# Second expert in a recurrence and mixture-of-experts kernel: three resident slabs in place of four streamed, with the planner's numbers set anew

## The chip, the cores and the metric

The kernel runs on one core of a Trainium2 chip. The metric is the device time of one execution in microseconds (us). Before the change three runs gave a median of 2320.58 us (2311.55 to 2326.86).

## What is computed

Three layers follow one another. The first is a recurrence over 768 tokens for 4 x 8 heads with a 40 x 40 state each, the second a mixture of eight experts whose weights P come from a Sinkhorn iteration over all 3072 tokens, the third one wide layer with an ELU. The reference, cut:

```python
for t in range(S):                                   # S = 768
    y[:, :, t] = np.einsum('bhd,bhde->bhe', rt, state)
    Sa = np.einsum('bhde,bhe->bhd', state, at)
    state_decay = state * wt[:, :, None, :] - np.einsum('bhd,bhe->bhde', Sa, bt)
    state = state_decay + np.einsum('bhd,bhe->bhde', vt, kt)
...
for e in range(E):                                   # 8 experts, D = 320, F = 1024
    h = np.maximum(x @ w1[e], 0.0)
    out += P[:, e:e + 1] * (h @ w2[e])
...
g = np.where(h > 0.0, h, alpha * (np.exp(np.minimum(h, 0.0)) - 1.0))   # h = x @ w_in, 2048 wide
return g @ w_out
```

## The kernel before

**Recurrence phase.** The 768 steps are cut into 12 chunks of 64 tokens (`NC`), and a chunk of all batches and heads gives 256 rows of x. A chunk is computed in matrix form on 16 head pairs in 4 groups. Its steps, in the names of the code: `scan`, `recip0` to `recip2`, `amul`, `bkmul` (VectorE and ScalarE); `gmm`, `at_t`, `kb_t` (TensorE); the inverse of a triangular matrix in 31 pairs `t_mul`, `t_add` on VectorE, which write the tiles TMP and U; then for each group in turn the state chain `y0mm` (R,SN), `qsmm` (matmul RHS,PT, then RHS<-bank,QM on VectorE), `ysmm` (matmul RHS,KB, then STMP, ST and Y on VectorE) and `trmm` (ident,ST). The matmul of the last group's `ysmm` ends a chunk: in this text the end of every fourth group of RHS,KB matmuls.

**Experts under the recurrence.** TensorE would have gaps in that chain, so the first experts' matmuls are put into them. An expert has 8 slabs of weights (128 of its 1024 hidden columns each, 352 KB). A slab is loaded by SP into one of two staging buffers `wst`, copied by ScalarE into one of 11 ring slots (`NSLOT`; tiles w), and the rest of the split into two planes is a subtraction that reads `wst` and the slot (line 596). This text calls one slab against the 256 rows of a chunk a **half step**: 8 matmuls of 256 columns (`mm1`), ReLU and split on ScalarE and VectorE (tiles hh, hl), and 6 matmuls of 320 columns each for one of two row blocks of 128, 12 in all for a full step on 512 rows (`mm2`). Expert 0 stays in slots 0 to 7 for all chunks (`moe0_items`). Of expert 1 slabs 0 to 3 are streamed for each of the chunks 0 to 9 through slots 8 to 10 (`moe1_items`, `stream_load`, `stream_split`, lists `STREAM` and `PASSES`): 40 loads, 40 copies on ScalarE and 40 subtractions on GpSimd. After chunk 9 the three slots are filled with slabs 0 to 2 once more, for the units: 3 of each again. Half steps per chunk: 8 and 4.

**What sets the order.** A planner (`class Order`) records each step's instructions, links them by the tiles they touch and sets the order of all engines ahead of time by a list schedule with prices for each instruction. Its ranks are moved by the table `AHEAD` and by `SLACK`, `FILL`, `FED` and `SAME`; the expert items (`item`) have a low rank on TensorE. When no expert item is open, it sets 128 x 128 matmuls on a tile of ones into gaps. Each engine then runs its instructions strictly in the order written. Expert items that the planner has not begun when the recurrence work is placed are kept in `left`.

**Behind the recurrence.** `moe0_rest` replays `left` and computes chunk 11's expert 0. The Sinkhorn steps hang in a queue `hookq` and are issued between matmuls by `tick`. As slots come free, `post_m2` puts `wsplit` of the slab 11 places on into the queue `late`; each pop issues a copy on ScalarE, a subtraction on GpSimd and the load of the next slab but one on SP. Then come the **units**: one slab against 512 rows (8 matmuls of 512 columns, 12 of 320), first what is left of expert 1, then experts 2 to 7 and the ELU layer in the same form (two sets): `units`, 8 + 5 x 4 = 28 for expert 1 and 384 for the other eight sets. The second matmuls of a unit run three units behind the first (`LAG`). `LEFT` lists the 512-row blocks whose earlier expert results are added from memory later on, 6 + 5.

Of the kernel before, what the change touches and what calls it, by code (L numbers as in the profile page):

```python
# [26 lines left out]
STREAM = [4, 4, 4, 4, 4]  # L27
PASSES = [f for c in range(10) for f in range(STREAM[c // 2])]
# [9 lines left out]
AHEAD = {"tnt": 60, "emm": 60, "t21": 20, "pmm": 60, "y0mm": 60, "qsmm": 60, "ysmm": 60, "trmm": -60, "st_copy": 60, "rvmm": 60, "load_vt": 60, "u_out": 60, "u_in": 60, "l_out": 20, "l_in": 100, "gmm": 40, "load_v": 20, "wsplit": -30}  # L38
# [15 lines left out]
class Order:  # L54
# [283 lines left out]
    SLACK, QUEUE, FILL, FED, SAME = 200.0, 1000.0, 0.0, 2000.0, 0.0  # L338
# [193 lines left out]
def kernel(  # L532
# [50 lines left out]
    wload_next, wlimit = [0], [NF - 1]  # L583

    def wload(i):
        while wload_next[0] <= min(i, wlimit[0]):
# [13 lines left out]
    def stream_load(k):  # L600
        if k < len(PASSES):
            SP.dma_start(out=wst[k % 2], in_=wslab[NF + PASSES[k]])

    def stream_split(k):
        if k < len(PASSES):
# [343 lines left out]
    def moe1_items(c):  # L949
        x = XS[c % 2]  # L950
        if c == 0:
            for k in range(2):
                stream_load(k)
            for k in range(3):
                stream_split(k)
                yield
        n = STREAM[c // 2]
        for f in range(n + 1):
            k = sum(STREAM[i // 2] for i in range(c)) + f
            if f < n:  # L960
# [384 lines left out]
```

## Time and profile before

| | us |
|---|---|
| median of the runs | 2320.58 |
| the profiled execution's own time | 2315.57 |
| its span | 2313.9 |
| TensorE busy | 2211.1 (96%) |
| VectorE busy | 1241.1 (54%) |
| ScalarE busy | 904.1 (39%) |
| GpSimd busy | 308.5 (13%) |

PE is TensorE, PEld its weight loads, DVE VectorE, ACT ScalarE, POOL GpSimd, SP the engine that issues nearly all transfers (SPq its queue). Times in the rows are us from the span's start. The profile gives one line (336) to all that the planner places, so its groups are told apart by the names of their tiles. A busy PE counts a matmul at a low clock as fully as one at a high clock; the granted clock (PEclk, 1.00 for the upper level of 2.4 GHz, 0.50 for the lower of 1.2) stands beside it.

### The profile page before, as it was taken

What the parts mean: (1) busy time and instruction counts of PE and PEld (TensorE: products, weight loads), DVE (VectorE), ACT (ScalarE), POOL (GpSimd) and SP (SyncE); (2) the same over time, 40 slices, a digit from 0 to 9 for tenths busy, and PEclk for the clock granted to TensorE, in tenths of its full rate; (3) what the DMA queues carried; (4) which work ended last, traced back from release to release, by engine and by line L of the source; (5) the groups of instructions that cost most, each with busy time, mean ns of one, the idle gap of its engine ahead of it and who ended that gap; (6) DMA issues with size and microseconds to landing.
All of it is one profiled execution on the core that took longest, in us unless ns stands there. A gap on an engine that the chain in (4) does not pass through costs nothing.

```text
span 2313.9 us, 42293 instructions
## 1 busy us (share of the span) xinstructions
PE 2211.1 (96%) x17586; PEld 1997.3 (86%) x17586; DVE 1241.1 (54%) x2518; ACT 904.1 (39%) x1897; POOL 308.5 (13%) x319
## 2 busy tenths in 40 slices
PE   6997999999999899999999999999999999999997
PEld 6876888888888889999999999999999998999997
DVE  7887477777775454556555432222222334556665
ACT  3554565565555222112112112112112224777665
POOL 2212222212221211002002002002002002001000
PEclk8877999999999899999999999999999999999999
DMA  3444444444443441113122101001001001000000
GB/s 100 111 127 109 122 119 130 121 123 126 118 119 89 140 132 47 61 61 110 61 61 88 38 23 51 1 1 51 1 1 51 1 1 51 1 1 20 19 24 29
DMA packets 171400, 152.65 MB, mean 66 GB/s; under 512 B 107648, under 2 KB 142336, under 8 KB 170240
## 3 DMA queue, kind: packets, MB, share of 16 engines
q1 hardware_dynamic: 170940, 149.53, 23.2%
q8 instruction: 140, 2.29, 0.4%
q14 instruction: 60, 0.49, 0.1%
q10 hardware_dynamic: 260, 0.33, 0.0%
HBM read 114.83 MB, written 35.00 MB: 65 GB/s over the span
## 4 chain that ended last, share of the span: by engine, by line
PE 85%; DVE 10%; issue 2%; ACT 1%; DMA 1%; POOL 0%; SPq 0%; DVEq 0%; ACTq 0%; POOLq 0%
PE bank L616 32%; PE bank L336 22%; PE bank L626 10%; PE bank L625 10%; PE bank L624 10%; DVE TMP L336 3%; DVE U L336 2%; DVE RHS L336 2%; DVE Y L336 0%; DVE ST L336 0%; DVE STMP L336 0%; PE bank L1149 0%; DMA wst<-in_wslab_dram 0%; DVE A L336 0%; ACT A L336 0%
## 5 line engine op out<-in xcount | busy, mean ns | idle before, releaser
L616 PE MATMUL bank<-X,w 128*128 128x512 f32 (+1 forms) x3360 | 829.6, 388 | 0.0
L616 PEld LDWEIGHTS bank<-X,w 128*128 128x128 f32 x3360 | 606.3, 188 | 103.4
L620 DVE SCALAR_TENSOR_TENSOR hl<-bank,hh 128x512 fp32r<-128x512 f32 x320 | 220.2, 689 | 607.7 <-ACT hh L619 607.6
L626 PE MATMUL bank<-w,hl 128*128 128x320 f32 x1664 | 515.0, 309 | 0.8 <-DVE hl L1143 0.8
L624 PE MATMUL bank<-w,hh 128*128 128x320 f32 x1664 | 514.0, 309 | 0.7 <-ACT hh L1142 0.7
L625 PE MATMUL bank<-w,hh 128*128 128x320 f32 x1664 | 514.3, 309 | 0.0
L619 ACT ACTIVATE hh<-bank 128x512 fp32r<-128x512 f32 x320 | 191.7, 599 | 814.0 <-PE bank L616 809.4
L624 PEld LDWEIGHTS bank<-w,hh 128*128 128x128 f32 x1664 | 313.3, 188 | 16.8 <-ACT hh L1142 1.1
L625 PEld LDWEIGHTS bank<-w,hh 128*128 128x128 f32 x1664 | 313.2, 188 | 15.6
L626 PEld LDWEIGHTS bank<-w,hl 128*128 128x128 f32 x1664 | 313.0, 188 | 1.3 <-DVE hl L1143 1.3
L596 POOL TENSOR_TENSOR w<-wst,w 128x704 fp32r<-128x704 f32 x69 | 118.6, 1720 | 1245.4 <-ACT w L595 1227.9
L336 PE MATMUL bank<-XS,w 128*128 128x256 f32 x1024 | 157.8, 302 | 0.0
L336 PEld LDWEIGHTS bank<-XS,w 128*128 128x128 f32 x1024 | 139.2, 202 | 6.2 <-issue 2.8
L369 DVE SCALAR_TENSOR_TENSOR NX<-EX,NX 128x512 f32<-128x512 f32 (+1 forms) x104 | 68.6, 660 | 135.0 <-ACT NX L368 134.6
L336 DVE TENSOR_TENSOR TMP<-U,LD 128x126 f32<-128x126 f32 (+22 forms) x372 | 133.2, 358 | 14.1 <-DMA BK<-in_wakb_dram 2.7
L336 PE MATMUL bank<-w,hh 128*128 128x320 f32 x512 | 126.3, 333 | 0.1
L336 DVE TENSOR_TENSOR U<-U,TMP 128x126 f32<-128x126 f32 (+22 forms) x372 | 111.8, 301 | 11.4
L1163 DVE SCALAR_TENSOR_TENSOR OUT<-bank,pp,OUT 128x320 f32<-128x320 f32 x144 | 69.2, 543 | 54.1 <-PE bank L626 54.1
L336 POOL TENSOR_TENSOR w<-wst,w 128x704 fp32r<-128x704 f32 x43 | 73.7, 1716 | 174.2 <-ACT w L336 88.5
L366 ACT ACTIVATE NX<-bank 128x512 f32<-128x512 f32 (+1 forms) x104 | 58.8, 565 | 83.6 <-PE bank L616 80.7
L336 DVE SCALAR_TENSOR_TENSOR hl<-bank,hh 128x512 fp32r<-128x512 f32 (+1 forms) x84 | 47.1, 560 | 78.8 <-ACT hh L336 78.5
L336 PEld LDWEIGHTS bank<-w,hh 128*128 128x128 f32 x512 | 85.2, 196 | 4.8 <-issue 2.1
(135 smaller groups left out, 2464.2 us busy)
## 6 DMA issues: line engine op xcount, KB each, us to landing
wst<-in_wslab_dram SPq DMA_DIRECT2D x104, 352.0 KB
RAW<-in_wslab_dram SPq DMA_DIRECT2D x32, 352.0 KB
BK<-in_wakb_dram SPq DMA_DIRECT2D x24, 320.0 KB
x_d<-XS SPq DMA_DIRECT2D x12, 640.0 KB
X<-x_d SPq DMA_DIRECT2D x12, 640.0 KB
ye_d<-YE SPq DMA_DIRECT2D x22, 320.0 KB
XS<-ye_d SPq DMA_DIRECT2D x11, 640.0 KB
LD<-l_d SPq DMA_DIRECT2D x24, 256.0 KB
```

The source lines that it names most:

```text
L336: getattr(self.engines[s.eng], method)(*args, **kwargs)
L366: nc.scalar.activation(out=n, in_=h, func=AF.Relu, scale=-1.0)
L369: nc.vector.scalar_tensor_tensor(out=n, in0=e, scalar=1.0, in1=n, op0=ALU.add, op1=ALU.mult)
L596: (V if i < NF else P).tensor_tensor(out=w[:, 1, :], in0=st, in1=fv(w[:, 0, :]), op=ALU.subtract)
L616: PE.matmul(ps, w[:, pl, c0:c0 + 128], x[:, m, :], start=(t == 0), stop=(t == 7))
L619: A.activation(out=h_hi, in_=ps, func=AF.Relu)
L620: V.scalar_tensor_tensor(out=h_lo, in0=ps, scalar=0.0, in1=fv(h_hi), op0=ALU.max, op1=ALU.subtract)
L624: PE.matmul(acc, h_hi, hi, start=first, stop=False)
L625: PE.matmul(acc, h_hi, lo, start=False, stop=False)
L626: PE.matmul(acc, h_lo, hi, start=False, stop=last)
L1163: V.scalar_tensor_tensor(out=o, in0=ps, scalar=pp[:, n, s:s + 1], in1=o, op0=ALU.mult, op1=ALU.add)
```

## The change

Slabs 0, 1 and 2 of expert 1 are loaded once into slots 8 to 10, with their subtraction on VectorE, and every chunk uses them: 3 half steps for each of the chunks 0 to 10 in place of 4 for chunks 0 to 9. Chunk 11's three half steps come behind the recurrence, in `moe0_rest`. Slabs 3 to 7 of expert 1 are then due for all six row blocks: 6 x 5 = 30 units in place of 28. The streaming code goes. `LEFT` has 12 entries. `AHEAD` (18 entries before, 27 after), `SLACK`, `FILL`, `FED` and `SAME` have new values. The diff, cut:

```diff
-STREAM = [4, 4, 4, 4, 4]
-PASSES = [f for c in range(10) for f in range(STREAM[c // 2])]
+KEPT = NSLOT - NF
...
-AHEAD = {"tnt": 60, "emm": 60, "t21": 20, "pmm": 60, ... "u_out": 60, "u_in": 60, "l_out": 20, "l_in": 100, "gmm": 40, ...}
+AHEAD = {"tnt": 80, "emm": 100, "t21": -30, ... "st_copy": 300, ... "u_out": 150, "u_in": 100, "l_out": 100, "l_in": 300, "gmm": 80, ...}
...
-    SLACK, QUEUE, FILL, FED, SAME = 200.0, 1000.0, 0.0, 2000.0, 0.0
+    SLACK, QUEUE, FILL, FED, SAME = 60.0, 1000.0, -100.0, 1000.0, 40.0
...
-        (V if i < NF else P).tensor_tensor(out=w[:, 1, :], in0=st, in1=fv(w[:, 0, :]), op=ALU.subtract)
+        (V if i < NSLOT else P).tensor_tensor(out=w[:, 1, :], in0=st, in1=fv(w[:, 0, :]), op=ALU.subtract)
...
-    def stream_split(k):
-        if k < len(PASSES):
-            st, w = wst[k % 2], wring[NF + k % 3]
-            A.copy(out=w[:, 0, :], in_=st)
-            P.tensor_tensor(out=w[:, 1, :], in0=st, in1=fv(w[:, 0, :]), op=ALU.subtract)
-            stream_load(k + 2)
...
     def moe1_items(c):
...
+        for f in range(KEPT + 1):
+            if f < KEPT:
                 for half in range(2):
-                    mm1(bank[f % 2][:, 0:256], wring[NF + k % 3], x, 4 * half, 4 * half + 4)
+                    mm1(bank[f % 2][:, 0:256], wring[NF + f], x, 4 * half, 4 * half + 4)
                     if half == 1:
                         relu_split(bank[f % 2][:, 0:256], hh[f % 2][:, 0:256], hl[f % 2][:, 0:256])
+                        if late:
+                            late.popleft()()
...
+                    if t == 1 and c == NC - 1:
+                        late.append(lambda ff=f - 1: post_m2(1, ff))
...
-                if k + 2 < len(PASSES):
-                    stream_split(k + 2)
...
-            for f in range(NF):
+            for f in range(NSLOT):
                 order.add(wsplit, f)
...
-            stream = chain(moe0_items(c), moe1_items(c) if c < 10 else ())
+            stream = chain(moe0_items(c), moe1_items(c))
...
-    LEFT = [(0, j) for j in FIRST] + [(1, j) for j in FIRST[1:]]
+    LEFT = [(e, j) for e in range(2) for j in FIRST]
...
         yield from moe0_items(NC - 1)
+        yield from moe1_items(NC - 1)
...
-    first = lambda s, j: STREAM[j] if s == 1 and j < 5 else 0
-    units = [(1, j, f) for j in FIRST for f in range(first(1, j), NF)]
+    first = lambda s: KEPT if s == 1 else 0
+    units = [(1, j, f) for j in FIRST for f in range(KEPT, NF)]
...
-        if s == 1 and j == 5 and f % 2 == 0:
-            load_x(f // 2 + 1)
+        if s == 1 and j == 5 and f - KEPT < 4:
+            load_x(f - KEPT + 1)
```

**The order on GpSimd, in the sixth chunk's state chain.** AFFINE_SELECT rows are the masks of `gmm` (GS) and `rvmm` (RHS); TENSOR_TENSOR rows are subtractions of slabs. Before, then of the change:

```order
64 L336 AFFINE_SELECT GS_124<-GS_124 64x4x64 x4
65 L336 AFFINE_SELECT RHS_140<-RHS_140 64x4x64
66 L336 AFFINE_SELECT RHS_141<-RHS_141 64x4x64
67 L336 AFFINE_SELECT RHS_140<-RHS_140 64x4x64
68 L336 AFFINE_SELECT RHS_141<-RHS_141 64x4x64
69 L336 AFFINE_SELECT GS_124<-GS_124 64x4x64 x4
70 L336 TENSOR_TENSOR w_90<-wst_94,w_90 128x704
71 L336 TENSOR_TENSOR w_91<-wst_93,w_91 128x704
72 L336 TENSOR_TENSOR w_92<-wst_94,w_92 128x704
73 L336 TENSOR_TENSOR w_90<-wst_93,w_90 128x704
```

```order
52 L335 AFFINE_SELECT RHS_140<-RHS_140 64x4x64
53 L335 AFFINE_SELECT RHS_141<-RHS_141 64x4x64
54 L335 AFFINE_SELECT RHS_140<-RHS_140 64x4x64
55 L335 AFFINE_SELECT RHS_141<-RHS_141 64x4x64
56 L335 AFFINE_SELECT RHS_140<-RHS_140 64x4x64 x2
57 L335 AFFINE_SELECT RHS_141<-RHS_141 64x4x64 x2
58 L335 AFFINE_SELECT GS_125<-GS_125 64x4x64 x8
59 L335 AFFINE_SELECT RHS_140<-RHS_140 64x4x64
```

In the change no subtraction of a slab stands on GpSimd before the recurrence has ended; the masks stay.

**The order on ScalarE just behind the recurrence**, in chunk 11's expert items. CAST rows copy a slab from staging (w_82 is slot 0, w_92 slot 10), ACTIVATE rows are ReLUs (128x512 two half steps of expert 0 or a unit, 128x256 one half step of expert 1), YE the results. Before, then of the change:

```order
756 L595 CAST w_84<-wst_94 128x704
757 L619 ACTIVATE hh_96<-bank_67 128x512
758 L595 CAST w_85<-wst_93 128x704
759 L945 COPY YE<-bank_68 128x320
760 L945 COPY YE<-bank_69 128x320
761 L619 ACTIVATE hh_95<-bank_66 128x512
762 L595 CAST w_86<-wst_94 128x704
763 L619 ACTIVATE hh_96<-bank_67 128x512
764 L595 CAST w_87<-wst_93 128x704
765 L619 ACTIVATE hh_8760<-bank_73 128x512
```

```order
705 L594 CAST w_85<-wst_93 128x704
706 L932 COPY YE<-bank_68 128x320
707 L932 COPY YE<-bank_69 128x320
708 L606 ACTIVATE hh_95<-bank_66 128x256
709 L594 CAST w_86<-wst_94 128x704
710 L606 ACTIVATE hh_96<-bank_67 128x256
711 L594 CAST w_87<-wst_93 128x704
712 L606 ACTIVATE hh_95<-bank_66 128x256
713 L594 CAST w_88<-wst_94 128x704
```

The copies of slots 4, 5 and 6 stood between the ReLUs of units; three now stand between the ReLUs of chunk 11's half steps of expert 1, whose second matmuls follow one half step behind, not three units.

**The order on SP at the same place.** X are the 512-row blocks for the units (X_8764 and X_8543 are block 0), wst the slab loads. Before, then of the change:

```order
342 L588 DMA wst_94<-in_wslab_dram 128x704
343 L588 DMA wst_93<-in_wslab_dram 128x704
344 L588 DMA wst_94<-in_wslab_dram 128x704
345 L588 DMA wst_93<-in_wslab_dram 128x704
346 L1081 DMA X_8764<-x_d 128x5x256 x2
347 L946 DMA ye_d<-YE 128x2x320
348 L1174 DMA RAW<-in_wslab_dram 128x704
```

```order
293 L587 DMA wst_94<-in_wslab_dram 128x704
294 L587 DMA wst_93<-in_wslab_dram 128x704
295 L1055 DMA X_8543<-x_d 128x5x256 x2
296 L587 DMA wst_94<-in_wslab_dram 128x704
297 L587 DMA wst_93<-in_wslab_dram 128x704
298 L933 DMA ye_d<-YE 128x2x320
299 L587 DMA wst_94<-in_wslab_dram 128x704
```

Block 0 now stands ahead of the third and fourth of these slab loads, where it stood behind the fourth.

## Rows read from the trace of the kernel before

**Rows 1.** The page: engines, busy tenths and clock in 40 slices, the chain.

```profile
PE 2211.1 (96%) x17586; PEld 1997.3 (86%) x17586; DVE 1241.1 (54%) x2518; ACT 904.1 (39%) x1897; POOL 308.5 (13%) x319
...
PE   6997999999999899999999999999999999999997
...
PEclk8877999999999899999999999999999999999999
...
PE 85%; DVE 10%; issue 2%; ACT 1%; DMA 1%; POOL 0%; SPq 0%; DVEq 0%; ACTq 0%; POOLq 0%
```

**Rows 2.** Stretches: length; PE, PEld, DVE, ACT, POOL busy (count); clock; DMA; GB/s.

```profile
0.00:101.60 101.60, 77.70 (x995) 70.76 (x995) 76.92 (x177) 43.07 (x113) 23.97 (x39) 0.83 0.41 105
101.60:150.40 48.80, 43.18 (x612) 37.20 (x612) 39.82 (x104) 25.35 (x69) 11.41 (x16) 0.91 0.51 124
...
292.10:714.30 422.20, 393.95 (x5292) 352.95 (x5292) 325.55 (x760) 238.32 (x618) 106.80 (x140) 0.95 0.46 121
714.30:762.20 47.90, 43.27 (x568) 38.26 (x567) 18.08 (x46) 22.89 (x55) 10.03 (x12) 0.90 0.33 90
762.20:802.90 40.70, 37.22 (x244) 36.34 (x245) 16.50 (x35) 11.15 (x23) 6.74 (x4) 0.87 0.40 124
802.90:2313.90 1511.00, 1493.48 (x8390) 1353.54 (x8389) 668.74 (x1197) 491.65 (x842) 111.82 (x65) 1.00 0.13 39
```

**Rows 3.** Timeline of PE: two half steps and the next start; two units' starts.

```profile
243.63 2.08 PE L336 MATMUL bank<-XS,w 128*128 128x256 f32 x16
245.54 0.46 PE L336 MATMUL bank<-w,hh 128*128 128x320 f32 x2
...
247.31 2.08 PE L336 MATMUL bank<-XS,w 128*128 128x256 f32 x16
```

**Rows 4.** Timeline of PE in the steady units: start us, us, what.

```profile
1003.03 2.00 PE L616 MATMUL bank<-X,w 128*128 128x512 f32 x8
...
1006.63 2.00 PE L616 MATMUL bank<-X,w 128*128 128x512 f32 x8
```

**Rows 5.** Tile w on POOL, 0 to 762.2: duration ns min/median/max, first and last start.

```profile
L336 POOL TENSOR_TENSOR w<-wst,w x43: 1666/1689/1876, 193.6 to 758.3; 128x704 fp32r<-128x704 f32 x43
```

**Rows 6.** Tile TMP (the inverse's pairs) on DVE, before and after the first such subtraction.

```profile
0.00:192.60 192.60, 55.74 (x193) 0.85 0.45 114
192.60:762.20 569.60, 189.29 (x551) 0.92 0.44 117
```

**Rows 7.** Tile RHS on DVE, 192.6 to 762.2: duration ns min/median/max.

```profile
L336 DVE TENSOR_TENSOR RHS<-bank,QM x76: 583/590/597, 200.0 to 759.9; 64x416 f32<-64x416 f32 x76
```

**Rows 8.** Timeline 186 to 230: POOL, then DVE, then PE [idle before, releaser].

```profile
193.65 3.32 POOL L336 TENSOR_TENSOR w<-wst,w 128x704 fp32r<-128x704 f32 x2 [0.95 <-DMA VE<-in_rv_dram]
...
193.83 1.60 DVE L336 TENSOR_TENSOR U<-U,TMP 128x78 f32<-128x78 f32 x1
195.46 1.68 DVE L336 TENSOR_TENSOR TMP<-U,LD 128x100 f32<-128x100 f32 x1
...
200.65 2.23 PE L336 MATMUL bank<-RHS,KB 128*40 128x104 f32 x16 [4.64 <-DVE RHS L336]
...
225.57 5.38 PE L336 MATMUL bank<-BK,AW 40*64 40x128 f32 x48 [6.37 <-DVE BK L336]
```

**Rows 9.** The stretches within 150 to 292, columns as in rows 2.

```profile
150.40:190.00 39.60, 38.87 (x570) 34.60 (x570) 27.98 (x47) 26.23 (x71) 10.39 (x14) 0.81 0.50 128
190.00:245.00 55.00, 39.39 (x328) 34.59 (x327) 39.38 (x88) 20.00 (x50) 17.06 (x17) 0.69 0.43 111
245.00:292.10 47.10, 44.00 (x598) 39.03 (x597) 28.15 (x70) 25.45 (x62) 10.29 (x12) 1.00 0.38 112
```

**Rows 10.** Timeline behind the recurrence: PE, then ACT.

```profile
759.95 2.23 PE L336 MATMUL bank<-RHS,KB 128*40 128x104 f32 x16 [0.75 <-DVE RHS L336]
...
794.24 0.60 PE L398 MATMUL bank<-sk,ones 128*128 128x8 f32 x2 [2.82 <-DVE sk L395]
...
815.50 0.78 ACT L595 CAST w<-wst 128x704 fp32r<-128x704 f32 x1 [6.06 <-DMA wst<-in_wslab_dram]
```

**Rows 11.** Groups by shape, 0 to 762.2: count, busy us, mean ns, idle before.

```profile
L336 ACT CAST w<-wst 128x704 fp32r<-128x704 f32 x51 | 39.5, 779 | 20.6 <-PE bank L336 14.1 <-DMA wst<-in_wslab_dram 5.5 <-issue 0.5
...
L336 DVE TENSOR_TENSOR w<-wst,w 128x704 fp32r<-128x704 f32 x8 | 7.1, 904 | 0.2 <-ACT w L336 0.2
```

More of the change, by code (lines that the diff above doesn't have):

```diff
@@ L35 @@
 EN = {"gmm": "PPPP", "rvmm": "PPPP", "qsmm": "VVVV"}
[L38 removed]
+AHEAD = {"tnt": 80, "emm": 100, "t21": -30, "y0mm": 20, "qsmm": 60, "ysmm": 100, "trmm": -60, "st_copy": 300, "rvmm": 60, "load_vt": 60, "u_out": 150, "u_in": 100, "l_out": 100, "l_in": 300, "gmm": 80, "wsplit": -30, "t_mul": 20, "t_add": 20, "at_t": 20, "kb_t": 150, "recip0": -30, "recip1": -60, "amul": 40, "x_in": -60, "xsplit": -60, "gatemm": 150, "load_r": -60}
 class Step:
@@ L580, in fv @@
         return ap.bitcast(F32)
-    wload_next, wlimit = [0], [NF - 1]
+    wload_next = [0]
     def wload(i):
-        while wload_next[0] <= min(i, wlimit[0]):
+        while wload_next[0] <= min(i, NSETS * NF - 1):
             n = wload_next[0]
@@ L595, in wsplit @@
         A.copy(out=w[:, 0, :], in_=st)
-        (V if i < NF else P).tensor_tensor(out=w[:, 1, :], in0=st, in1=fv(w[:, 0, :]), op=ALU.subtract)
+        (V if i < NSLOT else P).tensor_tensor(out=w[:, 1, :], in0=st, in1=fv(w[:, 0, :]), op=ALU.subtract)
         wload(i + len(wst))
-    def stream_load(k):
-        if k < len(PASSES):
-            SP.dma_start(out=wst[k % 2], in_=wslab[NF + PASSES[k]])
-    def stream_split(k):
-        if k < len(PASSES):
-            st, w = wst[k % 2], wring[NF + k % 3]
-            A.copy(out=w[:, 0, :], in_=st)
-            P.tensor_tensor(out=w[:, 1, :], in0=st, in1=fv(w[:, 0, :]), op=ALU.subtract)
-            stream_load(k + 2)
     TERMS = [(0, 0, 0), (0, 128, 1), (0, 0, 2), (0, 128, 3), (1, 0, 0), (1, 128, 1), (0, 256, 4), (1, 256, 4)]
@@ L950, in moe1_items @@
         x = XS[c % 2]
[L951 to L960, printed above, removed]
+        for f in range(KEPT + 1):
+            if f < KEPT:
                 for half in range(2):
-                    mm1(bank[f % 2][:, 0:256], wring[NF + k % 3], x, 4 * half, 4 * half + 4)
+                    mm1(bank[f % 2][:, 0:256], wring[NF + f], x, 4 * half, 4 * half + 4)
                     if half == 1:
                         relu_split(bank[f % 2][:, 0:256], hh[f % 2][:, 0:256], hl[f % 2][:, 0:256])
+                        if late:
+                            late.popleft()()
                     yield
@@ L968, in moe1_items @@
                     cs = slice(128 * t, 128 * t + 128)
-                    mm2(bank[2 + t][:, 0:320], hh[(f - 1) % 2][:, cs], hl[(f - 1) % 2][:, cs], wring[NF + (k - 1) % 3],
-                        f == 1, f == n)
-                    if t == 1 and f == n:
+                    mm2(bank[2 + t][:, 0:320], hh[(f - 1) % 2][:, cs], hl[(f - 1) % 2][:, cs], wring[NF + f - 1],
+                        f == 1, f == KEPT)
+                    if t == 1 and c == NC - 1:
+                        late.append(lambda ff=f - 1: post_m2(1, ff))
+                    if t == 1 and f == KEPT:
                         for tt in range(2):
@@ L975, in moe1_items @@
                     yield
-                if k + 2 < len(PASSES):
-                    stream_split(k + 2)
-                    yield
-        if c == 9:
-            wlimit[0] = NSETS * NF - 1
-            wload(NF + 1)
-            for n in range(NF, NSLOT):
-                wsplit(n)
-                yield
     late = deque()
@@ L1159, in evac @@
             ps, o, n = bank[2 + t][:, 0:320], OUT[j][:, t, :], 4 * j + t
-            if s == 1 or (s == 2 and first(1, j) == NF):
+            if s == 1:
                 V.tensor_scalar(out=o, in0=ps, scalar1=pp[:, n, s:s + 1], scalar2=None, op0=ALU.mult)
@@ L1230, in p2_m2 @@
             mm2(bank[2 + t0 + t][:, 0:320], hh[i % 4][:, ts], hl[i % 4][:, ts], wring[(s * NF + f) % NSLOT],
-                f == first(s, j), f == 7)
+                f == first(s), f == 7)
             if t % 2:
@@ L1238, in p2_m2 @@
                     hookq.append((10, lambda kt=kt: xt2(j, kt)))
-        if j == (4 if s == 1 and f >= STREAM[4] else 5):
+        if j == (4 if s == 1 else 5):
             late.append(lambda: post_m2(s, f))
```

## The prediction

> **What bounds the kernel now.** I read the page first. TensorE is busy for 96% of the span and holds 85% of the chain that ended last; the chain's next holder is VectorE with 10% [rows 1]. The clock digits are below 9 almost only in the first third. So I cut the span where the recurrence's last RHS,KB matmul ends, at 759.95 + 2.23 = 762.2 [rows 10], and asked for busy time by stretch [rows 2]. From 802.9 on, the units, TensorE is busy 1493.5 of 1511.0 us at clock 1.00: nothing is to be had there but by removing work. In the recurrence it is otherwise. Seven steady chunks (292.1 to 714.3) take 422.2 us, 60.3 each. TensorE idles 422.2 - 393.95 = 28.3 of it, and a mean clock of 0.95 is a tenth of the time at the lower level (1.2 in place of 2.4 GHz): 42 us, of which half, 21, are lost. VectorE is busy 77% there (325.6). The stretch 150.4 to 292.1, two chunks, takes 141.7 us, 70.9 each, and its middle, 190 to 245, shows 15.6 us of idle TensorE and a clock of 0.69 [rows 9].
>
> What late input makes these holes? In 186 to 230 TensorE waits 4.64 us for a VectorE result and then 6.37 for another [rows 8]. VectorE was not idle then: instructions of the inverse took 1.60 and 1.68 us. They lie on two GpSimd subtractions of streamed slabs (193.65, 3.32 us together). Six such long rows stand between 193 and 222; rows 8 has the first two.
>
> **The price of a stretched VectorE.** The inverse's instructions (tile TMP, written or read) are the same 62 in every chunk. Up to 192.6, ahead of the first subtraction of a slab on GpSimd, 193 of them took 55.74 us, 0.289 each; behind it 551 took 189.29, 0.344 each [rows 6]. The difference, 0.0547 x 551, is 30 us of VectorE time, over 43 subtractions of 1.67 to 1.88 us [rows 5]. The masking instruction RHS<-bank,QM, with one input in PSUM, keeps 583 to 597 ns over the same time [rows 7]: it is not every instruction. The Trainium skill, page "SBUF — State Buffer", section "Who interferes with whom", says that a VectorE instruction with two SBUF inputs and a GpSimd instruction that reads SBUF exclude each other for the whole instruction, and one with a single SBUF input is left alone; the rows agree on which are stretched. Taken at its worst it would hold VectorE for 43 x 1.69 = 73 us in place of the 30 measured, and the sum below would come out lower by 33 us at the same share passed on; I go by the 30.
>
> **The change part by part.**
>
> *Work on TensorE.* A half step's price: two of them take 247.31 - 243.63 = 3.68 us, 1.91 of it the first matmuls (245.54) [rows 3], so 1.84 each, 0.955 + 0.885. A unit's is 1006.63 - 1003.03 = 3.60 [rows 4]. Counted over the whole order, before the last RHS,KB group stand 120 first and 120 second halves in the old order, 112 and 110 in the new: -8 x 0.955 - 10 x 0.885 = -16.5 us in the recurrence. Behind it: 9 and 11 half steps left over in place of 8 and 8 (+3.6), chunk 11's three of expert 1 (+5.5), two more units (+7.2): +16.3. The sum is 0, as it must be: every slab still meets every row. The change can only move how TensorE waits.
>
> *Taken away at no price:* 40 of the recurrence's 51 slab loads, 14 MB, from a stretch whose DMA share is 0.46 [rows 2]; as many copies of 0.78 us on ScalarE [rows 11], which is busy 56% there. Both were covered by TensorE, so nothing is counted. Three slabs more are split on VectorE, 3 x 0.9 = 2.7 us [rows 11], spread over the first chunks where VectorE is 76 to 82% busy: below 1 us on the path. The twelfth `LEFT` addition, its load and four instructions lie in the units, where VectorE is busy 44% [rows 2].
>
> *A new wait behind the recurrence.* ScalarE's copies for slots 4 to 6 now stand between the ReLUs of chunk 11's half steps of expert 1, and SP loads X block 0 ahead of the first two of those slabs. In the old run such a copy sat 6.06 us for its load at 815.5 [rows 10] and cost nothing, since the units run three ahead. Here a late copy holds the next ReLU, and the second matmuls follow one half step behind (0.96 us of cover). Bounds: 0 if the loads are in time, 6 for one such wait passed on whole. I take 3: three copies at risk, of which SP's order delays two.
>
> *The stretch 190 to 245.* At the steady chunks' rate of idling (28.3/422.2) 55 us hold 3.7 us of idle; there are 15.6, so 12 too many. The clock of 0.69 means 34 us at the lower level; about 14 of them were idle anyway, so 20 us of work at half speed, 10 lost, against 2.7 usual: 7 too many. Together 19. The six stretched rows, each some 1.4 us over 0.289, give 8.4 of it directly, the rest is what idling did to the clock. I take 16 as gone with the subtractions; bounds 0 and 19.
>
> *The steady chunks.* 28 of the 43 subtractions fall there, so 30 x 28/43 = 20 us of stretched VectorE. A VectorE that is busy 77% passes on about that share of a delay: 15 us. Bounds: 0, and 49, all idle and low clock of those chunks (28 + 21).
>
> *The planner's new numbers.* What they do apart from this I put at 0, since no row prices them: in the new order each of chunks 4 to 11 carries 10 to 14 first halves of expert work, in the old 8 to 14.5, so TensorE is fed more evenly; but chunk 1 carries none (5.5 before) and 152 matmuls on ones are set in place of 123, so the plan has more gaps. Bounds: a third of the remaining idle and clock loss either way, some 12 us.
>
> Sum: 0 + 3 - 16 - 15 = -28 us. The profiled execution (span 2313.9, own time 2315.6) would come to about 2287.6. The median of the runs is 5 us above that execution; on it the forecast is 2320.6 - 28 = 2292.6.
>
> **Rivals.**
>
> *All of the waiting goes* (chance 0.17). Without the stretched VectorE the plan's order fits what happens, and most of the 49 us in the steady chunks, the 19 and the 4.6 idle in chunk 11 go: two thirds of 73 are -49, +3: 2275; down to 2255 if it is nearly all. For it: TensorE's holes have VectorE as releaser. Against: the first two chunks have no slab subtraction and still show clocks of 0.83 and 0.91 and 24 and 5.6 us idle [rows 2].
>
> *The stretched rows were covered* (0.24). Chunks 4 to 10 have stretched rows too and only 4.0 us idle each; if TensorE's queue of expert work hid them and the 190 to 245 hole comes of the old plan, the work moves one for one: 0 + 3, less up to 10, plus what an unlucky plan adds: 2310 to 2330, no change. In it TensorE's time per chunk falls by just the half steps.
>
> *Chunks paced by the chain, not by TensorE* (0.10). The other side: with one half step less per chunk TensorE is not the slower partner any more, the chunk keeps its 60.3 us, paced by VectorE and the state chain, and the work taken out of it is paid again behind: +16.3 + 3 to 6 = 2340 to 2343, more if added gaps let the clock fall. It decides if the chain's own pace is above 60.3 - 1.84 = 58.5 us. Against it: chunk 1, with 3.75 half steps and no subtraction, took 48.8 us at VectorE 82% busy [rows 2], so the pace is near 49. For it: VectorE's 46.5 us per steady chunk, a plan that needs fillers, and fewer expert items to put into gaps. The Trainium skill, page "TensorE: Matmul & The Clock Gate", section "Why this matters for your kernels", warns that idle gaps between bursts of matmuls bring the slow clock back. Rows 9 show it, 0.69 where 15.6 us were idle.
>
> The forecast itself has 0.49.
>
> **How the numbers follow.** The forecast's own range is 2280 to 2310: the share passed on from the steady chunks between 5 and 25, the new wait 0 to 6. 2262 leaves out the lower part of the first rival, 2330 the last rival: about 2 in 10 together. About 1% (23 us) is what a measurement of this kernel can tell from no change: faster means below 2297.4, slower above 2343.8. Faster: the first rival and two thirds of the forecast, 0.17 + 0.32 = 0.49. Slower: the upper part of the last rival, with stalls of its own, 0.08. Same: the rest, 0.43.
>
> **What would show it right or wrong.** The end of the last RHS,KB group shall come at 715 to 725 in place of 762, and the units' first matmul some 58 us behind it in place of 40.7. The inverse's instructions shall be back at 0.29 us each throughout, the longest near 0.48. Between 150 and 300 no wait of TensorE over 3 us shall have VectorE as releaser, and steady chunks shall take 55 to 57 us at a clock of 0.96 or more. In chunk 11's expert 1 a wait of TensorE for hl or hh of 3 to 6 us shall stand, with ScalarE waiting for wst. Wrong it is if VectorE's instructions shrink and the chunks do not (the second or third rival, told apart by whether a chunk takes 58.5 or 60), or if TensorE shows long waits at new places, which would be the plan's own doing.

## The result, and the profile after

The changed kernel takes 2249.96 us (median of 4 runs, 2249.48 to 2253.28) against 2318.73 us for the kernel before (4 runs, 2311.55 to 2326.86): a ratio of 0.9693, 95% interval 0.9661 to 0.9725. Forecast were 2292.6 us, range 2262 to 2330. The direction was right; the gain is 69 us where 28 were forecast, and the time lies below the range, and below that of the first rival ("all of the waiting goes", 2255 to 2275), which came nearest.

The profiled execution took 2249.76 us with a span of 2247.9. The page, lines as in [rows 1]:

```profile
PE 2188.1 (97%) x17628; PEld 1977.2 (88%) x17628; DVE 1220.3 (54%) x2523; ACT 880.7 (39%) x1859; POOL 232.0 (10%) x276
...
PE   8799999999998999999999999999999999999997
...
PEclk8899999999999999999999999999999999999999
...
PE 82%; DVE 12%; ACT 2%; issue 1%; DMA 1%; POOL 0%; SPq 0%; DVEq 0%; ACTq 0%; POOLq 0%
```

Behind the first two slices the clock digit is 9 everywhere; before, the third and fourth had 7 and a later one 8.

The stretches that answer to [rows 2] (chunks 0, 1, 2 to 3, 4 to 10, 11, the gap up to the units, the units, and chunks 2 to 11 together):

```profile
0.00:114.90 114.90, 91.81 (x1109) 82.25 (x1109) 86.52 (x195) 48.06 (x125) 27.29 (x49) 0.82 0.41 103
114.90:158.50 43.60, 39.27 (x614) 34.37 (x613) 40.26 (x100) 26.70 (x71) 6.71 (x7) 0.92 0.43 110
158.50:266.40 107.90, 105.09 (x1491) 94.06 (x1490) 91.64 (x220) 65.11 (x171) 24.75 (x36) 0.98 0.49 128
266.40:634.90 368.50, 361.88 (x5091) 322.58 (x5091) 293.84 (x735) 212.49 (x567) 51.18 (x109) 0.99 0.43 109
634.90:677.30 42.40, 42.40 (x593) 38.44 (x591) 15.20 (x32) 20.79 (x51) 3.25 (x8) 1.00 0.30 85
677.30:728.40 51.10, 45.88 (x317) 44.57 (x316) 27.70 (x60) 16.52 (x35) 11.59 (x7) 0.93 0.44 141
728.40:2247.90 1519.50, 1501.77 (x8427) 1360.93 (x8425) 665.18 (x1184) 490.99 (x841) 107.20 (x63) 1.00 0.13 38
158.50:677.30 518.80, 509.37 (x7171) 455.08 (x7169) 400.68 (x987) 298.38 (x789) 79.19 (x152) 0.99 0.43 111
```

The same sum of chunks 2 to 11 in the kernel before:

```profile
150.40:762.20 611.80, 559.49 (x7349) 499.44 (x7349) 439.13 (x1008) 332.88 (x853) 154.56 (x195) 0.92 0.44 117
```

Read the two together. The recurrence ends 84.9 us earlier (677.3 for 762.2). Chunks 0 and 1 lose 8.1 (158.5 for 150.4, with 116 matmuls more in them), chunks 2 to 11 win 93.0 (518.8 for 611.8), and what follows is 18.9 longer (1570.6 for 1551.7): 66.0, the difference of the spans. Of the 93.0, TensorE's idle time is 42.9 (52.3 falls to 9.4), and lost clock, counted as (1 - clock) x length and good to 3 us with two digits, 43.7 (48.9 falls to 5.2). The two counts overlap where TensorE idled at the lower level: by the trace's clock records 103.2 us of before's chunks 2 to 11 lie at that level, 17.9 of them idle, and 10.2 us of the change's, none idle. Work at the lower level alone, taken at half speed, thus lost an estimated 42.7 and 5.1 us, 37.5 less. The 12.6 us that remain are work that these chunks no longer hold: 178 matmuls fewer (7349 to 7171), of which chunks 0 and 1 have taken 116. So most of the gain is idle time and slow clock that went away, in about equal parts. The table below uses the two simple counts, overlap included.

### The profile page after: what moved, and what is told of

The parts are those of the page before. It is cut to its first block, busy times and chain, and to the rows that moved or that the text cites. A ratio compares the mean times of both kernels' runs of the same rounds, so it can differ in the third digit from the quotient of the medians.

```text
span 2247.9 us, 42203 instructions
## 1 busy us (share of the span) xinstructions
PE 2188.1 (97%) x17628; PEld 1977.2 (88%) x17628; DVE 1220.3 (54%) x2523; ACT 880.7 (39%) x1859; POOL 232.0 (10%) x276
## 4 chain that ended last, share of the span: by engine, by line
PE 82%; DVE 12%; ACT 2%; issue 1%; DMA 1%; POOL 0%; SPq 0%; DVEq 0%; ACTq 0%; POOLq 0%
PE bank L603 34%; PE bank L335 16%; PE bank L613 11%; PE bank L612 11%; PE bank L611 11%; DVE TMP L335 3%; DVE U L335 3%; DVE RHS L335 1%; DVE hl L335 1%; DVE A L335 0%; DVE Y L335 0%; PE bank L1124 0%; DVE WC L335 0%; ACT A L335 0%; DVE pp L393 0%
## 5 line engine op out<-in xcount | busy, mean ns | idle before, releaser
L607 DVE SCALAR_TENSOR_TENSOR hl<-bank,hh 128x512 fp32r<-128x512 f32 (+1 forms) x325 | 222.9, 687 | 614.5 <-ACT hh L606 614.5
L606 ACT ACTIVATE hh<-bank 128x512 fp32r<-128x512 f32 (+1 forms) x325 | 194.0, 597 | 827.4 <-PE bank L603 822.9
L595 POOL TENSOR_TENSOR w<-wst,w 128x704 fp32r<-128x704 f32 x69 | 118.8, 1722 | 1272.9 <-ACT w L594 1258.2
L335 PE MATMUL bank<-XS,w 128*128 128x256 f32 x968 | 142.0, 291 | 0.2 <-DVE XS L335 0.2
L335 DVE TENSOR_TENSOR TMP<-U,LD 128x126 f32<-128x126 f32 (+22 forms) x372 | 123.7, 333 | 16.6 <-DMA LD<-l_d 4.7
L335 PEld LDWEIGHTS bank<-XS,w 128*128 128x128 f32 x968 | 125.0, 191 | 5.5 <-issue 2.1
L335 DVE TENSOR_TENSOR U<-U,TMP 128x126 f32<-128x126 f32 (+22 forms) x372 | 99.3, 267 | 11.7
L335 POOL TENSOR_SCALAR_AFFINE_SELECT RHS<-RHS 64x256 f32<-64x256 f32 x96 | 49.1, 523 | 408.4 <-ACT RHS L335 406.9
L335 ACT COPY RHS<-bank 40x256 f32<-40x256 f32 (+1 forms) x192 | 70.4, 367 | 48.8 <-PE bank L335 43.4
```

The source lines that it names most:

```text
L335: getattr(self.engines[s.eng], method)(*args, **kwargs)
L595: (V if i < NSLOT else P).tensor_tensor(out=w[:, 1, :], in0=st, in1=fv(w[:, 0, :]), op=ALU.subtract)
L606: A.activation(out=h_hi, in_=ps, func=AF.Relu)
L607: V.scalar_tensor_tensor(out=h_lo, in0=ps, scalar=0.0, in1=fv(h_hi), op0=ALU.max, op1=ALU.subtract)
```

## The experiments

Three theories stood against each other. PORT: the 43 GpSimd subtractions stretch VectorE, and their removal is the gain. NUMBERS: the planner's new numbers are the gain. LOAD: one half step less per chunk is the gain. Lengths, idle and lost clock are those of chunks 2 to 11 in the profiled execution. "Numbers" are the planner's, old or new. Each ratio is taken against runs of the kernel before from the same session, whose medians lay between 2316.0 and 2319.3.

| run | structure; numbers | median us | ratio [95%] | length | idle | lost clock |
|---|---|---|---|---|---|---|
| before | streams; old | 2318.7 | 1 | 611.8 | 52.3 | 49 |
| e3_stream_no_sub | streams, no subtractions; old | 2298.7 | 0.991 [0.988, 0.994] | 584.1 | 33.2 | 35 |
| e9_stream_not_issued | no streaming work issued; old | 2294.7 | 0.989 [0.985, 0.993] | 587.4 | 29.9 | 47 |
| e6_four_resident_old | three kept, four half steps; old | 2279.8 | 0.984 [0.979, 0.988] | 574.7 | 16.4 | 17 |
| e1_kept_old_numbers | three kept; old | 2273.9 | 0.982 [0.978, 0.987] | 545.2 | 14.9 | 16 |
| after | three kept; new | 2250.0 | 0.969 [0.966, 0.973] | 518.8 | 9.4 | 5 |
| e7_four_resident_new | three kept, four half steps; new | 2256.9 | 0.975 [0.972, 0.978] | 535.2 | 8.7 | 21 |
| e2_stream_new_numbers | streams; new | 2381.1 | 1.025 [1.020, 1.030] | 646.0 | 70.2 | 78 |
| e8_stream_new_no_sub | streams, no subtractions; new | 2339.9 | 1.010 [1.007, 1.014] | 600.1 | 40.8 | 48 |
| e4_kept_gp_sub | three kept, 40 subtractions; new | 2284.9 | 0.985 [0.981, 0.989] | 552.8 | 31.8 | 17 |
| e5_kept_gp_memset | three kept, 120 memsets; new | 2252.1 | 0.972 [0.970, 0.975] | 518.4 | 10.1 | 5 |

e1, e2 and e3, and e10 and e14 further below, came out in none of the ranges written down ahead (e11 missed its own by 0.8 us): no one of the three theories holds alone.

Lengths compare only where the order is the same, since another order puts other work into chunk 11; medians compare always.

### Do the subtractions cost, and how much

**e3_stream_no_sub**, the old order with the subtractions left out:

```diff
+                if s.eng == "P" and method == "tensor_tensor":
+                    continue
...
```

> The kernel before with its own order on every engine, but GpSimd's 43 subtractions of slabs in the recurrence left out (the low planes of slots 8 to 10 are zeros there, so expert 1's results and those of the first units lack that part). Loads, copies and all matmuls stay. PORT expects the inverse's instructions at 0.29 us throughout, the last RHS,KB group at 700 to 725 in place of 762, and 2260 to 2285 us. NUMBERS and LOAD expect 2305 to 2320, since neither the order nor the half steps change.

**e4_kept_gp_sub**, the changed kernel with as much GpSimd reading put back:

```diff
+                if s.eng == "P" and method == "affine_select":
+                    self.masks += 1
+                    if self.masks > 32 and self.masks % 4 == 0:
+                        self.extra()
...
+    order.extra = lambda: P.tensor_tensor(out=SCR, in0=fv(wring[1][:, 0, 0:544]), in1=fv(wring[0][:, 0, 0:544]), op=ALU.subtract)
```

> The changed kernel in its own order with 40 more instructions on GpSimd, one behind every fourth mask from the 36th on: a subtraction of 544 columns of two ring slots into a tile that nobody reads, some 1.3 us each (estimated from the 1.69 us of one over 704 columns). PORT expects the inverse's instructions stretched by some 15 to 25 us in all and the time up by 15 to 40, 2265 to 2290. NUMBERS and LOAD expect 2248 to 2256.

**e5_kept_gp_memset**, the same places, GpSimd busy about as long, but only writing:

```diff
...
+        for _ in range(3):
+            P.memset(SCR, 0.0)
...
```

> The changed kernel in its own order with three memsets of 544 columns on GpSimd (about 1.5 us together, estimated from 0.97 us for a memset of 1040 columns at the program's start) at each of the 40 places where the run before had a subtraction. GpSimd is held as long, but reads nothing from SBUF. PORT expects 2250 to 2257, with the inverse's instructions unstretched. If what cost 35 us in the run with subtractions was that GpSimd's masks came later, it is 2275 to 2290 here too.

Chunks 2 to 11, all engines, and then the inverse's instructions alone (tile TMP on VectorE: length, busy and count, clock, DMA share, GB/s). First before and after, TMP only; before's whole row stands above:

```profile
150.40:762.20 611.80, 191.97 (x564) 0.92 0.44 117
```
```profile
158.50:677.30 518.80, 167.09 (x558) 0.99 0.43 111
```

e3, without subtractions:

```profile
151.80:735.90 584.10, 550.86 (x7350) 492.85 (x7349) 408.46 (x1008) 332.47 (x854) 81.89 (x152) 0.94 0.47 123
```
```profile
151.80:735.90 584.10, 165.66 (x564) 0.94 0.47 123
```

e4: its added line on GpSimd (duration in ns, minimum, median, maximum; first and last start), then the two stretches:

```profile
L1043 POOL TENSOR_TENSOR SCR<-w,w x40: 1324/1342/3480, 120.3 to 705.5; 128x544 bf16<-128x544 f32 x40
```
```profile
163.50:716.30 552.80, 521.02 (x7171) 463.31 (x7169) 429.89 (x986) 298.22 (x789) 130.56 (x190) 0.97 0.41 104
```
```profile
163.50:716.30 552.80, 187.39 (x558) 0.97 0.41 104
```

e5, the same (its chunk 1 ends at 161.2):

```profile
L1045 POOL MEMSET SCR<- x120: 542/552/817, 120.1 to 670.0; 128x544 bf16 x120
```
```profile
161.20:679.60 518.40, 508.27 (x7169) 453.78 (x7169) 401.02 (x987) 298.34 (x789) 139.08 (x266) 0.99 0.43 111
```
```profile
161.20:679.60 518.40, 167.11 (x558) 0.99 0.43 111
```

An instruction of the inverse takes 0.340 us with subtractions (before) and 0.294 without (e3); 0.299 in after, 0.336 with 40 subtractions put back (e4), 0.299 with memsets (e5). GpSimd was busier with the memsets (139.1 us) than with the subtractions (130.6), so it is their reading and not GpSimd's time that stretches VectorE. In the Trainium skill the page "SBUF — State Buffer", section "Who interferes with whom", says so too: a two-input VectorE instruction contends with a GpSimd instruction that reads SBUF, not with one that only writes it. The three runs agree.

The traces show where the time went. Of before's 744 instructions of the inverse, 45 overlap a subtraction, and these took 0.60 us more on average than others of their shape that overlap nothing on GpSimd, 27 us in all. In e5 the 56 that overlap a memset took 0.002 us more.

What it costs: in e3 VectorE is 30.7 us shorter (439.1 to 408.5) and the chunks 27.7, the median 19 to 20. In e4 VectorE is 29.2 us longer and the chunks 34.0, the median 35. A microsecond of stretched VectorE thus cost 0.65 to 1.2 us of the kernel. PORT holds for about 20 of the 69 us, in the order of before; with the new numbers under streaming, e2 to e8, the subtractions cost 41 (2381.1 - 2339.9), and VectorE is 43.7 us shorter. What they cost depends on the order around them.

### What of streaming costs besides

**e9_stream_not_issued** also leaves out the 43 copies and 45 loads:

```diff
+                name = kwargs["out"].tensor.name if "out" in kwargs else ""
+                if s.task.f is self.until and name.startswith("w"):
+                    continue
...
```

> The kernel before in its own order on every engine, with everything that streams left out in the recurrence: the 43 subtractions on GpSimd, the 43 copies on ScalarE and 45 loads on SP (slots 8 to 10 hold zeros, so expert 1's part of the result is wrong; all matmuls stay). Leaving out the subtractions alone gave 2299 us, a plan made without streaming 2280. If the copies and loads themselves hold the other engines, it is about 2280 or below; if the plan made around them is what costs the rest, it stays at 2292 to 2300.

4.0 us below e3, with intervals that overlap: copies and loads show no cost clear of the noise, as forecast.

**e6_four_resident_old** keeps four half steps per chunk, but plans without any streaming; slabs 0 to 2 are split on VectorE at the start, as in the change:

```diff
...
-            for k in range(2):
-                stream_load(k)
-            for k in range(3):
-                stream_split(k)
-                yield
...
-                if k + 2 < len(PASSES):
-                    stream_split(k + 2)
-                    yield
...
-            for n in range(NF, NSLOT):
-                wsplit(n)
-                yield
...
-            for f in range(NF):
+            for f in range(NSLOT):
```

> The kernel before with its numbers and its four half steps of expert 1 per chunk for ten chunks, but nothing is streamed: slots 8 to 10 hold slabs 0 to 2 throughout, and the fourth half step takes one of the three slots again (so expert 1's part of the result is wrong; the count of matmuls is that of before). The planner knows that there are no copies, loads and subtractions. LOAD (the half step less per chunk) expects 2300 to 2320, as before. If the burden of streaming is the cause, it comes out near the changed structure with old numbers, 2265 to 2285.

**e7_four_resident_new**: the same with both lines of new numbers.

> The same with the planner's new numbers. If the new numbers were bad for streaming because of the streaming's copies, loads and subtractions, this is 2245 to 2265, like the change. If they were bad because of four half steps per chunk, it is 2340 or more.

**e1_kept_old_numbers**: the changed kernel with both lines of numbers of before.

```diff
...
-    SLACK, QUEUE, FILL, FED, SAME = 60.0, 1000.0, -100.0, 1000.0, 40.0
+    SLACK, QUEUE, FILL, FED, SAME = 200.0, 1000.0, 0.0, 2000.0, 0.0
```

> Three theories for the 69 us. PORT: the subtractions of streamed slabs on GpSimd stretched VectorE's two-input instructions, and TensorE paid for it in waits and low clock. NUMBERS: the planner's new table and constants made an order with fewer waits, whatever is streamed. LOAD: three half steps of expert 1 per chunk in place of four leave TensorE room, whatever the rest. This kernel is the changed one with the planner's numbers of before. PORT and LOAD expect it at 2245 to 2270 us, since no slab is subtracted on GpSimd in the recurrence and the half steps are the new ones; NUMBERS expects it back at 2300 to 2320. Parts of both lie between.

e6 and e1 differ in the half steps per chunk (and in the units that take up the difference), and stand at 2279.8 (2269.3 to 2286.2) and 2273.9 (2273.3 to 2287.8); e7 and after, at 2256.9 and 2250.0. A half step less per chunk is worth 6 to 7 us by the medians, within the ranges of the runs for the first pair, so LOAD falls as the main cause. But from e9 to e6, which issue the same kinds of work in the recurrence with no slab streamed, 15 us go, 19 from e3. The intervals of e9 and e6 touch (0.985 to 0.993, 0.979 to 0.988), their runs don't (2287.3 to 2299.8, 2269.3 to 2286.2); those of e3 and e6 are apart. What differs is the order that the planner makes when no slab has to be split in the stream. One place shows it: the first matmuls of half steps in chunk 2 (8 make a half step; line, shapes, count, busy us, mean ns), in before, e3, e6 and after:

```profile
L336 PE MATMUL bank<-XS,w 128*128 128x256 f32 x33 | 7.6, 386 | 0.0
```
```profile
L338 PE MATMUL bank<-XS,w 128*128 128x256 f32 x33 | 7.9, 398 | 0.0
```
```profile
L336 PE MATMUL bank<-XS,w 128*128 128x256 f32 x64 | 10.3, 306 | 0.0
```
```profile
L335 PE MATMUL bank<-XS,w 128*128 128x256 f32 x76 | 11.1, 290 | 0.0
```

Chunk 2 got 4.1 half steps in the old order and 8 to 9.5 without streaming. Chunk 3 is the other way round; in before and after:

```profile
L336 PE MATMUL bank<-XS,w 128*128 128x256 f32 x148 | 23.2, 307 | 0.0
```
```profile
L335 PE MATMUL bank<-XS,w 128*128 128x256 f32 x104 | 15.3, 288 | 0.0
```

That is 18.5 and 13.0. The count alone doesn't say how much TensorE idles: before's chunk 3, with the most, idled 11.5 us, its chunk 2 8.0. TensorE's waits in these chunks, answering to [rows 8], in e3 (timeline, with idle before and releaser):

```profile
198.98 2.24 PE L338 MATMUL bank<-RHS,KB 128*40 128x104 f32 x16 [1.48 <-DVE RHS L338]
...
220.61 5.38 PE L338 MATMUL bank<-BK,AW 40*64 40x128 f32 x48 [4.54 <-DVE BK L338]
```

and the longest two of after between 150 and 300:

```profile
151.92 0.64 PE L335 MATMUL bank<-R,SN 40*40 40x64 f32 x16 [0.99 <-DVE Y L335]
...
215.51 0.42 PE L335 MATMUL bank<-w,hl 128*128 128x320 f32 x1 [0.70 <-DVE hl L335]
```

The two waits of 4.64 and 6.37 us shrink to 1.48 and 4.54 with the subtractions gone, and are gone in the order of after, where no BK,AW group waits for VectorE. In e6's, RHS holds TensorE for 0.25 us at most there, and 2.82 us stand ahead of one BK,AW group without a releaser in the profile. That it is the expert work at these places that covers them is argued from the orders, not tried by itself. Chunks 2 and 3:

```profile
150.40:292.10 141.70, 122.26 (x1492) 108.22 (x1492) 95.51 (x204) 71.68 (x182) 37.74 (x43) 0.83 0.43 116
```
```profile
151.80:284.90 133.10, 122.08 (x1493) 108.20 (x1492) 85.82 (x204) 71.62 (x183) 19.36 (x32) 0.85 0.47 123
284.90:688.10 403.20, 385.41 (x5293) 346.42 (x5293) 304.63 (x761) 238.08 (x618) 59.17 (x112) 0.97 0.49 126
```
```profile
156.60:271.60 115.00, 108.20 (x1485) 97.53 (x1485) 94.06 (x219) 63.39 (x171) 25.60 (x32) 0.91 0.44 114
```

Before (first), e3 (second fence, with its chunks 4 to 10) and e6 (third): 141.7, 133.1, 115.0, with TensorE at nearly the same number of matmuls.

### The numbers

**e2_stream_new_numbers**, the kernel before with both lines of new numbers, and **e8_stream_new_no_sub**, the same without the subtractions (e3's edit):

```diff
...
-    SLACK, QUEUE, FILL, FED, SAME = 200.0, 1000.0, 0.0, 2000.0, 0.0
+    SLACK, QUEUE, FILL, FED, SAME = 60.0, 1000.0, -100.0, 1000.0, 40.0
```

> The kernel before, streaming four slabs past each chunk, with the planner's new numbers. NUMBERS expects 2250 to 2270. PORT and LOAD expect 2290 to 2325, since all 43 subtractions stay on GpSimd (the inverse's instructions at 0.33 to 0.35 us each behind the first of them) and the half steps are the old ones.

> The kernel before with the new numbers (2381 us) in the order that the planner made, but with the 43 subtractions on GpSimd left out (low planes of slots 8 to 10 are zeros). PORT alone expects 20 to 40 us less, 2340 to 2360. If all of the 131 us to the change were the stretching, it would be near 2260; if the order itself is the cause, it stays above 2335.

The same numbers win 24 us on the kept slabs (e1 to after, 2273.9 to 2250.0; e6 to e7, 23) and lose 63 on the streamed ones (2318 to 2381); without the subtractions they still lose 41 (2298.7 to 2339.9). Chunks 2 to 11 of e2 and e8:

```profile
169.70:815.70 646.00, 575.83 (x7283) 514.84 (x7283) 445.32 (x993) 328.41 (x833) 155.87 (x192) 0.88 0.42 109
```
```profile
172.50:772.60 600.10, 559.28 (x7284) 500.99 (x7283) 401.66 (x993) 327.95 (x833) 80.77 (x152) 0.92 0.45 118
```

So neither "the numbers" nor "the structure" has a price of its own: they fit each other.

Four constants change (QUEUE stays at 1000). Five runs split the numbers; each takes or gives only the named part.

**e10_kept_new_table**: after with the old constants.

> The changed kernel with the new table AHEAD, but SLACK, FILL, FED and SAME of before. With all old numbers it was 2274, with all new ones 2250. If the table (inverse chain's transfers and state copies first) makes the difference: 2250 to 2258. If the constants make it: 2266 to 2276.

**e11_kept_new_consts**: after with the old AHEAD table.

> The reverse: the old table with the new SLACK, FILL, FED and SAME. If the constants (TensorE no longer held back 0.2 us for a step of higher rank, and kept on matmuls of one shape) make the difference: 2250 to 2260; if the table does: 2266 to 2276.

**e13_kept_old_slack60**: after with all old numbers but SLACK at 60.

> The changed structure with the old numbers (2274 us) but SLACK 60 in place of 200: the planner may hold an engine back for a step of higher rank by 0.06 us and no longer by 0.2. All four new constants together gave 2261. If SLACK is what counts among them: 2256 to 2266. If not: 2270 to 2278.

**e14_kept_old_same40**: after with all old numbers but SAME at 40.

> The changed structure with the old numbers but SAME 40 in place of 0: a step of the same matmul shape as the last gets a better rank on TensorE. If SAME is what counts: 2256 to 2266; if not: 2270 to 2278. The count of shape changes on TensorE was 388 with the old numbers and 403 with the new constants, which speaks against it.

**e15_stream_new_consts**: the kernel before with the new constants and its own table.

> The kernel before, streaming, with the new constants and its own table. With both new it was 2381, with none 2318. If the table alone is what did not go with streaming (it also gave 2319 on the changed structure without the constants): 2300 to 2318. If the constants do not go with streaming either: 2325 to 2370.

| run | median us | ratio [95%] | length | idle | lost clock |
|---|---|---|---|---|---|
| e10 | 2318.5 | 1.000 [0.998, 1.002] | 594.9 | 24.8 | 54 |
| e11 | 2260.8 | 0.975 [0.971, 0.979] | 537.8 | 11.0 | 16 |
| e13 | 2265.3 | 0.977 [0.973, 0.980] | 549.4 | 14.1 | 11 |
| e14 | 2285.5 | 0.986 [0.981, 0.990] | 564.5 | 19.2 | 17 |
| e15 | 2352.8 | 1.015 [1.011, 1.019] | 648.0 | 69.9 | 71 |

From e1 (2273.9), SLACK alone gives -9, SAME alone +12 (with runs that overlap e1's), the four constants together -13, the table alone +45, and constants and table together -24. So the same table costs 45 us beside the old constants and gains 11 beside the new ones (e11 to after). On the streaming kernel the constants alone cost 34 (2318.7 to 2352.8). Effects that change sign with what stands beside them are no sum of causes: each set of numbers is another order, and some orders leave fewer holes (idle 9.4 us in after, 24.8 in e10, 70.2 in e2). Why these numbers place the streamed splits so badly is open.

### The waits that are left behind the recurrence

**e12_kept_sinkhorn_early** starts the Sinkhorn steps seven steps of the loop earlier and puts each sum two steps later:

```diff
-    return [(0, sk0), (8, sk1), (3, sk2)] + [(5, sk_row), (11, sk_sum), (3, sk_col)] * 8
+    return [(0, sk0), (8, sk1), (3, sk2)] + [(5, sk_row), (13, sk_sum), (3, sk_col)] * 8
...
-        if n > 11:
+        if n > 4:
```

> The changed kernel with its Sinkhorn steps begun seven items earlier behind the recurrence and the column sums' matmuls issued 13 ticks behind the row step in place of 11. In the changed kernel TensorE waits some 6.9 us there for VectorE's row step, and the clock falls to the lower level three times between 714 and 742. If these waits hold TensorE: 2243 to 2248 us. If the waits only move to the next thing that is late: 2249 to 2252.

The group of column sums between 677 and 760 in after, and in e12 (last: idle before, releaser):

```profile
L397 PE MATMUL bank<-sk,ones 128*128 128x8 f32 x16 | 2.8, 247 | 6.9 <-DVE sk L394 6.9
```
```profile
L397 PE MATMUL bank<-sk,ones 128*128 128x8 f32 x16 | 2.8, 249 | 2.9 <-DVE sk L394 2.9
```

4.0 us of waiting for the column sums go and the time stays: 2250.69 (2250.30 to 2252.41), ratio 0.9703 [0.967, 0.974]. The wait has moved. In e12 TensorE waits for a half step's low plane (hl) in chunk 11's expert 1, where after has no such wait:

```profile
727.69 0.64 PE L613 MATMUL bank<-w,hl 128*128 128x320 f32 x1 [3.50 <-DVE hl L607]
```

All of TensorE's waits between 677 and 760 come to 7.9 us in after and 8.2 in e12. No run beats the changed kernel.

## Why the prediction was right or wrong

**The work on TensorE (0 net): right, as far as the runs show.** The part behind the recurrence was forecast 19.3 us longer (16.3, and 3 for the new wait) and is 18.9 longer: 10.4 up to the units and 8.5 in them, for 12.1 and 7.2.

**Loads and copies at no price: right, within the noise** (e9 against e3).

**The new wait (+3, bounds 0 to 6): 0.** ScalarE did wait for slabs in chunk 11's expert 1, at the first two rows here, but for 1.89 and 0.73 us, and no second matmul waited for it:

```profile
710.12 0.78 ACT L594 CAST w<-wst 128x704 fp32r<-128x704 f32 x1 [1.89 <-DMA wst<-in_wslab_dram]
...
713.03 0.78 ACT L594 CAST w<-wst 128x704 fp32r<-128x704 f32 x1 [0.73 <-DMA wst<-in_wslab_dram]
```

What TensorE waits for there is the Sinkhorn sum, which the step did not name; such waits stood already in [rows 10]. The first unit starts 51.1 us behind the recurrence's end, not 58; the forecast's own terms up to there (3.6, 5.5 and 3 on 40.7) make 52.8.

**The price of the subtractions (-31 in all: 16 at 190 to 245, 15 in the steady chunks): too high by the medians, with a wrong split.** e3 takes out just them. Its profiled chunks 2 and 3 are 8.6 us shorter (141.7 to 133.1) and its steady chunks 19.0 (422.2 in [rows 2] to 403.2), 27.6 together; its median is 20 lower (the profiled execution was the fastest of five). The steady chunks passed on nearly all of the 20 us of stretch, not 77%. The hole at 190 to 245 was for the larger part not the subtractions': 8.6 in place of 16, which is just the step's direct part (8.4); what it added for the clock did not come. The step took VectorE's being the releaser for the cause. VectorE is late there in e3 too, without a subtraction, by 4.54 us at BK; in the order of after no such wait is left.

**The planner at 0, bounds 12 either way: the step that failed.** It put what the planner does, apart from the other terms, at 0 "since no row prices them". Two things stand behind that, the plan made for a structure without streamed splits, which had no term of its own, and the new numbers; both left the bounds. With no slab to split in the stream, the same old numbers give a more even order: 15 to 19 us (e9 or e3 to e6), and 6 more with one half step less (e1), the last within the ranges of the runs. The new numbers give 24 more (e1 to after). Together with the subtractions' 20 that is the 69: 2318.7 to 2298.7 (e3), to 2273.9 (e1), to 2250.0. The middle value leans on e1, whose fourth run took 2287.8; by means the three parts are 22, 20 and 27. They hold along this path alone: in another order, from before to e2, e8 and after, the numbers cost 62, leaving out the subtractions gives 41, and the new structure with its plan gives 90. The observation was there in the step itself ("TensorE is fed more evenly"), read from the order, but only for chunks 4 to 11 and chunk 1. The uneven place is chunks 2 and 3, 4.1 and 18.5 half steps in the old order, 9.5 and 13.0 in the new, and there lay 19.4 of before's 52.3 us of idle time. Chunk 2 and chunk 3 of before:

```profile
150.40:211.10 60.70, 52.74 (x721) 45.43 (x722) 47.45 (x94) 34.42 (x92) 16.26 (x19) 0.76 0.45 118
211.10:292.10 81.00, 69.53 (x772) 62.80 (x772) 48.05 (x111) 37.26 (x91) 21.47 (x24) 0.87 0.43 114
```

Why an order with these numbers leaves fewer holes is open; what is shown is that the order alone makes 24 us (e1 to after) and most of the 25 before that.

And the bounds were too narrow for what an order can do: e2 and e10, with an idle plus lost clock of 148 and 78 us, show that a planner's numbers reach far beyond a third of what was left.

**The rivals.** "All of the waiting goes" came nearest, but by the wrong means: it let all of it go with the stretched VectorE, which e3 refutes (68 us of idle and lost clock stay, by the table's counts). "The stretched rows were covered" falls: they cost 20. "Chunks paced by the chain" falls: the steady chunks take 52.6 us each (368.5 / 7), well below 58.5, with 6.6 us idle in all seven.

**The signs.** The last RHS,KB group ends at 677.3 (forecast 715 to 725), and steady chunks take 52.6 us at 0.99 (forecast 55 to 57 at 0.96 or more): both beyond. No wait over 3 us for VectorE between 150 and 300: so. The inverse's instructions are at 0.299, not quite 0.29, and the longest takes 0.556 us, not 0.48:

```profile
L335 DVE TENSOR_TENSOR TMP<-U,LD x279: 179/346/556, 174.6 to 630.7; 128x126 f32<-128x126 f32 x13, 128x30 f32<-128x30 f32 x8, 128x56 f32<-128x56 f32 x8, 128x78 f32<-128x78 f32 x8
```

GpSimd's masking stays in the recurrence (POOL is busy 79.2 us there), and the trace puts the rest down to it: 132 of after's 744 instructions of the inverse overlap a mask, and these took 0.063 us more on average than others of their shape that overlap nothing on GpSimd, 8.3 us in all. No run takes the masks out.

## What to carry to other kernels

When an edit takes operations out of a planned, in-order schedule, price three things apart: the operations' own interference (leave them out with the order held), the plan made without them, and the plan's numbers. Along the path taken here they were 20, 25 and 24 us, and only the first could be read from the durations of before. The engine that releases a long wait need not be its cause: with the subtractions gone, 4.54 of the 6.37 us at BK stayed, and the order of after had no such wait. A count of the cover (here half steps) per chunk doesn't find such places, since before's chunk 3 had the most and idled longest; where in the chunk it stands has to be looked at. And planner numbers are tuned for one structure: these won 24 us on the new one and lost 63 on the old.

## What the runs showed of the hardware

**Idle time and slow clock went together.** From before to after 42.9 us of idle time went, and with it 43.7 us of lost clock (37.5 without the idle part of it), so that between these two kernels a wait cost about twice its length. One instance stands in after, behind a Sinkhorn sum that came 1.85 us late: matmuls of the same shape go from 0.31 to 0.47 us, and stay there until 717.5. The granted clock is 1.00 from 713.5 to 714.1 and 0.51, the lower level, from 714.1 to 717.5.

```profile
713.46 0.39 PE L397 MATMUL bank<-sk,ones 128*128 128x8 f32 x2 [1.85 <-DVE sk L394]
...
713.93 0.31 PE L612 MATMUL bank<-w,hh 128*128 128x320 f32 x1
...
714.51 0.47 PE L612 MATMUL bank<-w,hh 128*128 128x320 f32 x1
...
717.67 0.31 PE L612 MATMUL bank<-w,hh 128*128 128x320 f32 x1
```

The ratio isn't fixed: e4 has 22 us more idle than after and 11 more lost clock, e7 0.7 less idle and 16 more lost clock.

**GpSimd's memset left VectorE alone** (0.299 us per instruction with and without 120 of them), where reading subtractions of about the same total time took it to 0.336. A mask (AFFINE_SELECT, which reads and writes its tile) did stretch those it overlapped, by 0.063 us on average.
